# A fused S5 and SwiGLU layer: three input tiles on one queue, gate weights in three pieces, and a re-ordered first layer norm

## The chip, the cores and the metric

The kernel runs on one core of a Trainium2 chip. The metric is device time in microseconds (us) of one execution. The kernel before took 180.87 us (median of 4 runs, 180.3 to 181.23). The one execution that the profile was taken from took 181.51 us; its span, from the first to the last instruction, is 179.8 us, so 1.7 us lie around the span.

## What is computed

The input x is 2048 rows of 512 values in bfloat16. A layer norm over each row gives xn. The output is x plus two branches of xn:

```
xn  = layernorm(x)                                   # 2048 x 512
A   = 2 * Re(scan(B_bar xn)) @ C  + xn * Dskip       # complex diagonal recurrence over the 2048 rows, 512 states
B   = (silu(xn @ w_gate) * (xn @ w_up)) @ w_down     # 512 -> 1376 -> 512
out = x + A + B
```

## The kernel before, in words

The 2048 rows are 16 tiles of 128 rows, and four tiles make a chunk of 512 rows. TensorE needs xn transposed (features on partitions). For chunks 1 to 3 one DMA transpose per chunk does that (`xTd1` to `xTd3`, L556). For chunk 0 it is done by hand, so that TensorE can begin early:

- `ln_chunk0` (L509) normalises tiles 0 to 3 on VectorE. Per tile: two `bn_stats` on 256 columns each (`bn_half`, L500), one `bn_aggr` (L513), a square root on ScalarE (`sd`, L515), a reciprocal (L519), and the normalised tile in two halves of 256 columns (`ln_half`, L505). The chain of `order=(last,)` fixes the order on VectorE by hand: the first half statistics of tile a+1 stand ahead of the reciprocal of tile a, the second half statistics of tile a+1 behind both normalised halves of tile a.
- `xt_tile_fine` (L539) transposes one half tile with two TensorE transposes (L546) and copies the result to SBUF on ScalarE (`xTev`, L552).
- `ffn_gate_quarters` (L737) computes the first six 128-column blocks of the gate product for chunk 0, one quarter (one tile of 128 rows) at a time, two of the four K blocks per step (L760). The two transposes of tile q+1 stand inside quarter q, ahead of steps 8 and 10 of 12. Ahead of quarter 0 stand warm-up matmuls on a constant (L457).

After that come the up product of the same blocks (`ffn_up`, L715, evacuated by ScalarE at L785), the remaining gate and up blocks, the recurrence input (`ssm_b_chunk`, L832), and for each chunk the down product (L915) and the output product of the recurrence (L928). The recurrence itself runs on VectorE (L863 and L872). Its cos and sin tables and parameters are made in the first third (`params_a`, `params_b`, `tables`, L610 to L677).

Inputs come through DMAs that all go through `dma` (L378, issued at L387 or, for transposes, L382). SyncE issues nearly all of them in program order. Before the change ScalarE issues two: tile 1 of x and the first half of the gate weights (`ld_x1`, `ld_wgA0`). A DMA transpose waits for every DMA before it, and every DMA after a transpose waits for that transpose (L381, L385). So SyncE's queue is a serial chain once the first loads are done: two transposes of B, the transpose of chunk 1, two transposes of C, and only then the load of x for chunk 2 (`ld_x8`, L428).

The order of instructions on ScalarE, VectorE and GpSimd is not the program's. `_schedule` (L79) plays the program through with the cost `est` that each operation is given, and a DMA model of 330 bytes per ns and 2000 ns. At each step it takes the operation that can start first, or, among those within 200 ns of it, the one with the longest remaining chain (`bl`). TensorE and SyncE keep program order (`_CHAIN`). An `order` edge fixes a sequence without a semaphore. The order so planned is then fixed in the program, whatever the true times are.

The layer norm of chunk 2 is on this path: the statistics (L470, L474) on VectorE, `ve` and `rstd` on GpSimd (L478, L482), `nmr` on VectorE (L491), and the normalised tiles 8 to 11 on ScalarE (`xn8` to `xn11`, L494).

Of the kernel before, what the change touches and what calls it, by code (L numbers as in the profile page):

```python
# [14 lines left out]
AF = mybir.ActivationFunctionType  # L15
# [63 lines left out]
def _schedule(tasks, engines, slack=200.0):  # L79
    succ = defaultdict(list)  # L80
    for t in tasks:
        for d in t.deps | t.od:
            succ[d].append(t)
    chain_next = {}
    for eng in _CHAIN:
        lst = [t for t in tasks if t.eng == eng]
        for a, b in zip(lst, lst[1:]):
            chain_next[a] = b
    for t in tasks:
        t.lat = (_DMA_LAT + t.nbytes / _DMA_BW) if t.dma else 0.0  # L90
    for t in reversed(tasks):
# [12 lines left out]
    chain_pos = {e: 0 for e in _CHAIN}  # L104
    for e in engines:
        if e in _CHAIN:
            continue
        ready[e] = [t for t in remaining[e] if nun[t] == 0]
    free = {e: 0.0 for e in engines}
    dma_free = {e: 0.0 for e in engines}  # L110
    order = {e: [] for e in engines}
    left = len(tasks)
    done = set()

    def est_start(t, e):
        s = free[e]
        for d in t.deps:
            f = d.fin + _HOP
            if f > s:
                s = f  # L120
        return s

    while left:
        best = None
        for e in engines:
            if e in _CHAIN:
                lst = remaining[e]
# [110 lines left out]
def bass_parallel_sum__ssm_conv_s5__swiglu_ffn__prompt_kernel(  # L238
# [30 lines left out]
    g = _Graph()  # L269
    es = ExitStack()  # L270
    with es:
# [123 lines left out]
        TILEB = 128 * D * 2  # L395
        FH0 = 6 * 128

        def pload(name, slot, src):
            return dma(name, prow[4 * slot:4 * slot + 4, :], src.rearrange("(a p) -> a p", p=128), [("prow", slot)], 1024)
# [4 lines left out]
        def wg_load(h, **kw):  # L404
            return dma("ld_wgA%d" % h, wg[:, 2 * h:2 * h + 2, 0:FH0], wg_v[:, 2 * h:2 * h + 2, 0:FH0], [("wg", "a%d" % h)], 256 * FH0 * 2, **kw)
# [92 lines left out]

        def bn_half(a, h, order=()):
            return g.add("dve", lambda e: e.bn_stats(out=st0[:, a, h, :], in_=x_sb[:, a, h * 256:(h + 1) * 256]),  # L500
                         reads=[("x", a)], writes=[("st0", a, h)], name="bnst%d_%d" % (a, h), est=330, order=order)

        def ln_half(a, h, order=()):
            cs = slice(h * 256, (h + 1) * 256)
# [1 line left out]
                                                          op0=ALU.subtract, op1=ALU.mult),  # L506
                         reads=[("x", a), ("mv", a), ("rstd", a)], writes=[("xh", a, h)] + ([("xn", a % NXN)] if h else []), name="xn%d_%d" % (a, h), est=220, order=order)

        def ln_chunk0():  # L509
            last = bn_half(0, 0)  # L510
            for a in range(4):
                last = bn_half(a, 1, order=(last,))
                last = g.add("dve", lambda e, a=a: e.bn_aggr(out=mv[:, a, :], in_=st0[:, a].rearrange("p h s -> p (h s)")),  # L513
                             reads=[("st0", a, 0), ("st0", a, 1)], writes=[("mv", a)], name="bnag%d" % a, est=130, order=(last,))
                hold["sd"] = g.add("act", lambda e, a=a: e.activation(out=sd0[:, a:a + 1], in_=mv[:, a, 1:2], func=AF.Sqrt, bias=epst[:, 0:1]),  # L515
                                   reads=[("mv", a), ("epst",)], writes=[("sd0", a)], name="sd%d" % a, est=280)
                if a < 3:
                    last = bn_half(a + 1, 0, order=(last,))
                last = g.add("dve", lambda e, a=a: e.reciprocal(out=rstd[:, a:a + 1], in_=sd0[:, a:a + 1]), reads=[("sd0", a)], writes=[("rstd", a)],  # L519
                             name="rstd%d" % a, est=100, order=(last,))  # L520
# [18 lines left out]
        def xt_tile_fine(a, hs=(0, 1)):  # L539
            for h in hs:  # L540
# [13 lines left out]
                hold["evac"] = g.add("act", evac, reads=BK(slot), writes=[("xnTh", a, h)] + ([("xnT", 0, a % 4)] if h else []), name="xTev%d_%d" % (a, h), est=340)  # L554

        def xt_chunk_dma(c):  # L556
            s0 = (4 * c) % NXN
# [140 lines left out]

        def wres(nm, i):
            if nm == "wg" and i < 6:  # L700
                return [("wg", "a0"), ("wg", "a1")]
            return [(nm, 0 if i < 6 else 1)]

        FP = [(0, 2), (2, 2), (4, 2), (6, 2), (8, 2)]
# [32 lines left out]
        def ffn_gate_quarters(pairs):  # L737
# [2 lines left out]
            banks = {ip: next_pair() for ip in pairs}  # L740
            tiles = [(2 * ip + k, banks[ip] + k) for ip in pairs for k in range(2)]
            wbank, pbk = tiles[-2][1], tiles[-1][1]
            pe_warm(10, 512, wbank)
            ln_chunk0()
            xt_tile_fine(0, (0,))
            pe_warm(1, 256, wbank)
            xt_tile_fine(0, (1,))
            pe_warm(3, 128, wbank)
            for q in range(4):
                if q < 3:  # L750
                    steps = [(i, bk, 2 * kh, 2 * kh + 2) for kh in range(2) for i, bk in tiles]
                else:
                    steps = [(i, bk, 2 * kh, 2 * kh + 2) for kh in range(2) for i, bk in tiles[:2]] + [(i, bk, 0, 4) for i, bk in tiles[2:]]
                for n, (i, bk, k0, k1) in enumerate(steps):
                    if q < 3 and n in (8, 10):
                        xt_tile_fine(q + 1, ((n - 8) // 2,))

                    def mm(e, bk=bk, i=i, q=q, k0=k0, k1=k1):
                        for kt in range(k0, k1):
                            inst = e.matmul(pbank[:, bk, q * 128:(q + 1) * 128], lhsT=wg[:, kt, i * 128:(i + 1) * 128], rhs=xnT[:, 0, q, kt, :],  # L760
                                            start=(kt == 0), stop=(kt == KT - 1))
                        return inst
                    hs = range(k0 // 2, k1 // 2)
# [3 lines left out]
                    g.add("pe", mm, reads=[("wg", "a%d" % h) for h in hs] + [("xnTh", q, h) for h in hs], writes=BK(bk), name="mm_gq%d_%d_%d" % (i, q, k0),  # L767
                          est=(k1 - k0) * 56, ninst=k1 - k0)
            reserved.clear()
            act_table(AF.Silu, (hold["evac"],))  # L770
# [277 lines left out]
```

## Time and profile before

| what | value |
|---|---|
| median of 4 runs | 180.87 us (180.3 to 181.23) |
| the profiled execution | 181.51 us, span 179.8 us |
| busy in the span | TensorE 174.8 us (97%), VectorE 161.9 us (90%), ScalarE 89.4 us (50%) |
| first gate matmul | 7.40 us |
| first up matmul | 14.03 us |
| granted TensorE clock | 1.0 as the mean of the span |

How to read it: times are microseconds from the start of the span. PE is TensorE, PEld its weight loads, DVE VectorE, ACT ScalarE, POOL GpSimd, SP SyncE. An entry of a timeline gives the start, the time from the first start to the last end of the merged instructions, the engine, the line, the operation, output and input, the count, and in brackets how long the engine was idle before it and what ended that. TensorE's instructions overlap in a pipeline, so the time of a row of N matmuls is read from the starts of this row and the next.

### The profile page before, as it was taken

The numbers are of one execution on the slowest core, as the hardware profiler recorded it, in microseconds if no ns is written. First come the engines' busy times: TensorE is split into PE (matmuls) and PEld (weight loads), VectorE is DVE, ScalarE is ACT, GpSimd is POOL, SyncE is SP. The second block draws the span as 40 slices with busy tenths as digits, with TensorE's granted clock in tenths as the row PEclk, the third lists the DMA queues.
The fourth block names the chain that finished last, engine by engine and source line by source line (L and its number), as shares of the span: only waits on it lengthen the run. The fifth ranks groups of instructions, "written<-read, shape, count | busy, mean of one in ns | idle before, by whom it ended". The sixth has DMA issues, their size and how long they took to land.

```text
span 179.8 us, 2391 instructions
## 1 busy us (share of the span) xinstructions
PE 174.8 (97%) x917; PEld 83.5 (46%) x925; DVE 161.9 (90%) x280; ACT 89.4 (50%) x116; POOL 9.9 (6%) x21
## 2 busy tenths in 40 slices
PE   8799999999999999999999999999999999999994
PEld 2585444444444444444444444444444444444743
DVE  2759895697799999999999999999999999999983
ACT  3369989989799966106656552000865620000000
POOL 3005400000500000040000000000000000000000
PEclk9999999999999999999999999999999999999999
DMA  5993677569541000001250000001100000000122
GB/s 177 358 327 62 108 103 113 115 133 360 175 94 26 0 0 0 0 0 62 81 95 0 0 0 4 0 0 58 58 0 4 0 0 0 0 0 4 58 80 95
DMA packets 22882, 12.37 MB, mean 69 GB/s; under 512 B 15096, under 2 KB 22872, under 8 KB 22872
## 3 DMA queue, kind: packets, MB, share of 16 engines
q1 hardware_dynamic: 22456, 11.70, 25.4%
q10 hardware_dynamic: 416, 0.52, 0.9%
q8 instruction: 7, 0.11, 0.3%
q14 instruction: 3, 0.02, 0.1%
HBM read 6.46 MB, written 2.10 MB: 48 GB/s over the span
## 4 chain that ended last, share of the span: by engine, by line
PE 93%; DMA 3%; ACT 1%; issue 0%; ACTq 0%; DVE 0%
PE pb L715 35%; PE pb L915 21%; PE pb L832 15%; PE pb L928 15%; DMA wg<-in_B_w_gate_dram 3%; PE pb L760 3%; PE pb L795 2%; PE pb L805 1%; ACT xn_sb L494 1%; ACT uf L785 1%; PE pb L546 0%; ACTq L387 0%; DVE x_sb L933 0%; PE pb L462 0%
## 5 line engine op out<-in xcount | busy, mean ns | idle before, releaser
L872 DVE TENSOR_TENSOR_SCAN rot<-sm,car,rot 128x512 bf16<-128x512 f32 x32 | 39.0, 1266 | 0.1
L915 PE MATMUL pb<-wd,hT 128*128 128x512 bf16 (+3 forms) x194 | 38.1, 355 | 0.2
L715 PE MATMUL pb<-xnT,wu 128*128 128x512 bf16 x160 | 37.3, 379 | 0.1
L715 PE MATMUL pb<-xnT,wg 128*128 128x512 bf16 x136 | 32.0, 379 | 0.0
L928 PE MATMUL pb<-W,hss 128*128 128x512 bf16 (+2 forms) x140 | 28.1, 355 | 0.2
L832 PE MATMUL pb<-xnT,BT 128*128 128x512 bf16 x128 | 28.1, 379 | 0.0
L915 PEld LDWEIGHTS pb<-wd,hT 128*128 128x128 bf16 (+1 forms) x198 | 18.5, 98 | 19.9
L715 PEld LDWEIGHTS pb<-xnT,wu 128*128 128x128 bf16 x160 | 15.5, 98 | 19.1 <-ACT uf L785 0.6
L727 ACT ACTIVATE sg<-pb 128x1024 bf16<-128x1024 f32 x20 | 20.2, 1023 | 7.6 <-PE pb L715 7.5
L785 ACT ACTIVATE uf<-pb 128x1024 bf16<-128x1024 f32 x20 | 20.4, 1026 | 7.0 <-PE pb L715 6.8
L715 PEld LDWEIGHTS pb<-xnT,wg 128*128 128x128 bf16 x136 | 13.1, 98 | 16.4 <-issue 0.8
L928 PEld LDWEIGHTS pb<-W,hss 128*128 128x128 bf16 x144 | 13.5, 98 | 14.3
L832 PEld LDWEIGHTS pb<-xnT,BT 128*128 128x128 bf16 x128 | 12.5, 98 | 15.1
L839 ACT ACTIVATE u_sb<-pb 128x1024 bf16<-128x1024 f32 x16 | 16.4, 1025 | 4.8 <-PE pb L832 4.5
L787 DVE TENSOR_TENSOR hT<-sg,uf 128x1024 bf16<-128x1024 bf16 x20 | 13.3, 680 | 0.4 <-ACT uf L785 0.3
L863 DVE TENSOR_TENSOR rot<-u_sb,cosT 128x2048 bf16<-128x2048 bf16 x8 | 9.7, 1218 | 2.9 <-ACT cosT L676 2.9
L933 DVE TENSOR_TENSOR x_sb<-pb,x_sb 128x512 bf16<-128x512 f32 (+2 forms) x18 | 10.8, 622 | 1.3 <-PE pb L928 1.3
L814 ACT ACTIVATE sg<-pb 96x1024 bf16<-96x1024 f32 x2 | 2.0, 1020 | 17.3 <-PE pb L795 17.3
L494 ACT ACTIVATE xn_sb<-x_sb,nmr,rstd 128x512 bf16<-128x512 bf16 x8 | 5.9, 802 | 9.3 <-DVE nmr L491 9.3
L863 DVE TENSOR_TENSOR rot<-rot,cosT 128x2048 bf16<-128x2048 bf16 x8 | 9.7, 1217 | 0.1
L863 DVE TENSOR_TENSOR rot<-rot,sin 128x2048 bf16<-128x2048 bf16 x8 | 9.7, 1218 | 0.0
L863 DVE TENSOR_TENSOR rot<-u_sb,sin 128x2048 bf16<-128x2048 bf16 x8 | 9.7, 1217 | 0.0
(76 smaller groups left out, 142.7 us busy)
## 6 DMA issues: line engine op xcount, KB each, us to landing
out_dram<-x_sb SPq DMA_DIRECT2D x15, 128.0 KB, 1.7
x_sb<-in_A_x_dram SPq DMA_DIRECT2D x3, 512.0 KB, 7.5
wd<-in_B_w_down_dram SPq DMA_DIRECT2D x1, 1280.0 KB, 7.1
wu<-in_B_w_up_dram SPq DMA_DIRECT2D x1, 768.0 KB, 5.7
wg<-in_B_w_gate_dram SPq DMA_DIRECT2D x1, 608.0 KB, 7.1
wu<-in_B_w_up_dram SPq DMA_DIRECT2D x1, 608.0 KB, 8.2
x_sb<-in_A_x_dram SPq DMA_DIRECT2D x3, 128.0 KB, 3.3
wg<-in_B_w_gate_dram ACTq DMA_DIRECT2D x1, 384.0 KB, 6.0
```

The lines of the kernel that those rows point to most:

```text
L494: g.add("act", lambda e, a=a: e.activation(out=xn_sb[:, a % NXN, :], in_=x_sb[:, a, :], func=AF.Identity, scale=rstd[:, a:a + 1], bias=nmr ...
L715: inst = e.matmul(pbank[0:fs, bk, :].rearrange("p (j t) -> p j t", j=4), lhsT=w[:, kt, i * 128:i * 128 + fs], rhs=xnT[:, c % 2, :, kt, :], ...
L727: g.add("act", lambda e: e.activation(out=sg[rows, sl, 0:n, :].rearrange("p a t -> p (a t)"), in_=pair_f32(rows, bk, 512 * n), func=AF.Sil ...
L785: g.add("act", lambda e: e.activation(out=uf[rows, ul, 0:n, :].rearrange("p a t -> p (a t)"), in_=pair_f32(rows, bk, 512 * n), func=AF.Ide ...
L787: g.add("dve", lambda e: e.tensor_tensor(out=hT[rows, hb, i0:i0 + n, :], in0=sg[rows, sl, 0:n, :], in1=uf[rows, ul, 0:n, :], op=ALU.mult), ...
L832: inst = e.matmul(pbank[:, bk, :].rearrange("p (j t) -> p j t", j=4), lhsT=BT[:, ri, kt, pt * 128:(pt + 1) * 128], rhs=xnT[:, c % 2, :, kt ...
L839: g.add("act", lambda e: e.activation(out=u_sb[:, us].rearrange("p r t -> p (r t)"), in_=pair_f32(slice(0, 128), b0), func=AF.Identity), r ...
L863: tt = lambda out, a, b, op, r, w, nm: g.add("dve", lambda e: e.tensor_tensor(out=out, in0=a, in1=b, op=op), reads=r, writes=w, name="%s_% ...
L872: g.add("dve", lambda e, A0=A0, A1=A1, k=k, ri=ri, pt=pt: e.tensor_tensor_scan(out=A1[:, k, ri, :], data0=rr[:, pt:pt + 1].to_broadcast([1 ...
L915: inst = e.matmul(pbank[:, bk, 0:nc_], lhsT=hT[0:fs, hb, i, lt * 128:(lt + 1) * 128], rhs=wd[0:fs, i, c0:c0 + nc_], start=(i == 0), stop=F ...
L928: inst = e.matmul(pbank[:, bk, 0:nc_], lhsT=hss[:, hb, pt, ri, lt * 128:(lt + 1) * 128], rhs=W12[:, ri, pt, c0:c0 + nc_], start=False, sto ...
L933: g.add("dve", lambda e, bk=bk, a=a, c0=c0, nc_=nc_: e.tensor_tensor(out=x_sb[:, a, c0:c0 + nc_], in0=pbank[:, bk, 0:nc_], in1=x_sb[:, a, ...
```

## The change

It has five parts.

1. Tile 1 of x moves from ScalarE's queue to SyncE's, behind tile 0.
2. ScalarE's queue now begins with the small load of `log_dt` (1 KB), then K blocks 0 and 1 of the gate weights (384 KB), then K block 2 (192 KB). K block 3 (192 KB) is on SyncE behind tile 2. Before, blocks 2 and 3 were one load of 384 KB on SyncE. Quarter 0 of the gate product takes K blocks 2 and 3 in separate steps (18 steps in place of 12), and tile 1's transposes stand ahead of steps 12 and 15.
3. Tile 0's statistics are one `bn_stats` on 512 columns. On VectorE the second half statistics and the aggregation of tile a+1 now stand ahead of the second normalised half of tile a, and the first half statistics of tile a+2 behind it.
4. On ScalarE, by `order` edges: `sd1` ahead of the copy of tile 0's second half, `sd2` behind the copy of tile 1's second half, `sd3` behind the copy of tile 2's second half.
5. The first warm-up is nine matmuls of 512 columns and two of 128 in place of ten of 512. Four costs that the planner is given rise (330 to 350, 130 to 160, 100 to 140 ns; 640 for the full statistics). `_schedule` walks the graph in topological order, since an edge can now point to an operation made earlier.

```diff
-            return dma("ld_wgA%d" % h, wg[:, 2 * h:2 * h + 2, 0:FH0], ...)
+            return dma("ld_wg" + nm, wg[:, k0:k1, 0:FH0], wg_v[:, k0:k1, 0:FH0], [("wg", nm)], (k1 - k0) * 128 * FH0 * 2, **kw)
         x_load(0)
-        act_q = [x_load(1, eng="act")]
-        act_q.append(wg_load(0, eng="act", order=(act_q[-1],)))
+        x_load(1)
+        act_q = [pload("ld_ldt", 2, A_log_dt, eng="act")]
+        act_q.append(wg_load("a0", 0, 2, eng="act", order=(act_q[-1],)))
         x_load(2)
-        wg_load(1)
+        act_q.append(wg_load("a1", 2, 3, eng="act", order=(act_q[-1],)))
+        wg_load("a2", 3, 4)
         x_load(3)
-        pload("ld_ldt", 2, A_log_dt)
...
+        def ln_stat0(a, order):
+            t = g.add("dve", lambda e: e.bn_aggr(out=mv[:, a, :], in_=st0[:, a].rearrange("p h s -> p (h s)")[:, 0:6 if a == 0 else 12]),
+                      reads=[("st0", a, 0), ("st0", a, 1)], writes=[("mv", a)], name="bnag%d" % a, est=160, order=order)
+            hold["sd%d" % a] = g.add("act", lambda e: e.activation(out=sd0[:, a:a + 1], in_=mv[:, a, 1:2], func=AF.Sqrt, bias=epst[:, 0:1]), ...)
+            return t
         def ln_chunk0():
-            last = bn_half(0, 0)
+            last = g.add("dve", lambda e: e.bn_stats(out=st0[:, 0, 0, :], in_=x_sb[:, 0, :]), reads=[("x", 0)], writes=[("st0", 0, 0)], name="bnst0", est=640)
+            last = ln_stat0(0, (last,))
+            last = bn_half(1, 0, order=(last,))
             for a in range(4):
...
-                if a < 3:
-                    last = bn_half(a + 1, 0, order=(last,))
-                last = g.add("dve", lambda e, a=a: e.reciprocal(...), est=100, order=(last,))
-                for h in range(2):
-                    last = ln_half(a, h, order=(last,))
+                last = g.add("dve", lambda e, a=a: e.reciprocal(...), est=140, order=(last,))
+                last = ln_half(a, 0, order=(last,))
+                if a < 3:
+                    last = bn_half(a + 1, 1, order=(last,))
+                    last = ln_stat0(a + 1, (last,))
+                last = ln_half(a, 1, order=(last,))
+                if a < 2:
+                    last = bn_half(a + 2, 0, order=(last,))
...
-                hold["evac"] = g.add("act", evac, ..., est=340)
+                hold["evac"] = g.add("act", evac, ..., est=340,
+                                     order=(hold["sd1"],) if (a, h) == (0, 1) else ())
+                if (a, h) in ((1, 1), (2, 1)):
+                    hold["sd%d" % (a + 1)].od.add(hold["evac"])
...
-            pe_warm(10, 512, wbank)
+            pe_warm(9, 512, wbank)
+            pe_warm(2, 128, wbank)
...
-                if q < 3:
+                if q == 0:
+                    steps = [(i, bk, 0, 2) for i, bk in tiles] + [(i, bk, k, k + 1) for k in (2, 3) for i, bk in tiles]
+                elif q < 3:
...
-                    if q < 3 and n in (8, 10):
-                        xt_tile_fine(q + 1, ((n - 8) // 2,))
+                    if q < 3 and n in ((12, 15) if q == 0 else (8, 10)):
+                        xt_tile_fine(q + 1, (0 if n in (8, 12) else 1,))
```

More of the change, by code (lines that the diff above doesn't have):

```diff
@@ L90, in _schedule @@
         t.lat = (_DMA_LAT + t.nbytes / _DMA_BW) if t.dma else 0.0
-    for t in reversed(tasks):
+    nin = defaultdict(int)
+    for t in tasks:
+        for d in succ[t]:
+            nin[d] += 1
+    for d in chain_next.values():
+        nin[d] += 1
+    topo = [t for t in tasks if nin[t] == 0]
+    for t in topo:
+        for d in succ[t] + ([chain_next[t]] if t in chain_next else []):
+            nin[d] -= 1
+            if nin[d] == 0:
+                topo.append(d)
+    for t in reversed(topo):
         b = 0.0
@@ L396, in bass_parallel_sum__ssm_conv_s5__swiglu_ffn__prompt_kernel, with pload, wg_load @@
         FH0 = 6 * 128
-        def pload(name, slot, src):
-            return dma(name, prow[4 * slot:4 * slot + 4, :], src.rearrange("(a p) -> a p", p=128), [("prow", slot)], 1024)
+        def pload(name, slot, src, **kw):
+            return dma(name, prow[4 * slot:4 * slot + 4, :], src.rearrange("(a p) -> a p", p=128), [("prow", slot)], 1024, **kw)
         def x_load(a, **kw):
             return dma("ld_x%d" % a, x_sb[:, a:a + 1, :], x_v[:, a:a + 1, :], [("x", a)], TILEB, **kw)
-        def wg_load(h, **kw):
-            return dma("ld_wgA%d" % h, wg[:, 2 * h:2 * h + 2, 0:FH0], wg_v[:, 2 * h:2 * h + 2, 0:FH0], [("wg", "a%d" % h)], 256 * FH0 * 2, **kw)
+        def wg_load(nm, k0, k1, **kw):
+            return dma("ld_wg" + nm, wg[:, k0:k1, 0:FH0], wg_v[:, k0:k1, 0:FH0], [("wg", nm)], (k1 - k0) * 128 * FH0 * 2, **kw)
         x_load(0)
-        act_q = [x_load(1, eng="act")]
-        act_q.append(wg_load(0, eng="act", order=(act_q[-1],)))
+        x_load(1)
+        act_q = [pload("ld_ldt", 2, A_log_dt, eng="act")]
+        act_q.append(wg_load("a0", 0, 2, eng="act", order=(act_q[-1],)))
         x_load(2)
-        wg_load(1)
+        act_q.append(wg_load("a1", 2, 3, eng="act", order=(act_q[-1],)))
+        wg_load("a2", 3, 4)
         x_load(3)
-        pload("ld_ldt", 2, A_log_dt)
         pload("ld_lim", 1, A_Lambda_im)
@@ L500, in bn_half @@
             return g.add("dve", lambda e: e.bn_stats(out=st0[:, a, h, :], in_=x_sb[:, a, h * 256:(h + 1) * 256]),
-                         reads=[("x", a)], writes=[("st0", a, h)], name="bnst%d_%d" % (a, h), est=330, order=order)
+                         reads=[("x", a)], writes=[("st0", a, h)], name="bnst%d_%d" % (a, h), est=350, order=order)
         def ln_half(a, h, order=()):
@@ L507, in ln_half @@
                          reads=[("x", a), ("mv", a), ("rstd", a)], writes=[("xh", a, h)] + ([("xn", a % NXN)] if h else []), name="xn%d_%d" % (a, h), est=220, order=order)
+        def ln_stat0(a, order):
+            t = g.add("dve", lambda e: e.bn_aggr(out=mv[:, a, :], in_=st0[:, a].rearrange("p h s -> p (h s)")[:, 0:6 if a == 0 else 12]),
+                      reads=[("st0", a, 0), ("st0", a, 1)], writes=[("mv", a)], name="bnag%d" % a, est=160, order=order)
+            hold["sd%d" % a] = g.add("act", lambda e: e.activation(out=sd0[:, a:a + 1], in_=mv[:, a, 1:2], func=AF.Sqrt, bias=epst[:, 0:1]),
+                                     reads=[("mv", a), ("epst",)], writes=[("sd0", a)], name="sd%d" % a, est=280)
+            return t
@@ L509, in ln_chunk0 @@
         def ln_chunk0():
-            last = bn_half(0, 0)
+            last = g.add("dve", lambda e: e.bn_stats(out=st0[:, 0, 0, :], in_=x_sb[:, 0, :]), reads=[("x", 0)], writes=[("st0", 0, 0)], name="bnst0", est=640)
+            last = ln_stat0(0, (last,))
+            last = bn_half(1, 0, order=(last,))
             for a in range(4):
[L512 to L516, printed above, removed]
-                if a < 3:
-                    last = bn_half(a + 1, 0, order=(last,))
-                last = g.add("dve", lambda e, a=a: e.reciprocal(out=rstd[:, a:a + 1], in_=sd0[:, a:a + 1]), reads=[("sd0", a)], writes=[("rstd", a)],
-                             name="rstd%d" % a, est=100, order=(last,))
-                for h in range(2):
-                    last = ln_half(a, h, order=(last,))
@@ new lines, in ln_chunk0 @@
+                last = g.add("dve", lambda e, a=a: e.reciprocal(out=rstd[:, a:a + 1], in_=sd0[:, a:a + 1]), reads=[("sd0", a)], writes=[("rstd", a)],
+                             name="rstd%d" % a, est=140, order=(last,))
+                last = ln_half(a, 0, order=(last,))
+                if a < 3:
+                    last = bn_half(a + 1, 1, order=(last,))
[3 more added lines that the diff above has]
+                    last = bn_half(a + 2, 0, order=(last,))
@@ L553, in evac @@
                                         in_=ptr[:, slot, 0:256].rearrange("p (k t) -> p k t", k=2), func=AF.Identity)
-                hold["evac"] = g.add("act", evac, reads=BK(slot), writes=[("xnTh", a, h)] + ([("xnT", 0, a % 4)] if h else []), name="xTev%d_%d" % (a, h), est=340)
+                hold["evac"] = g.add("act", evac, reads=BK(slot), writes=[("xnTh", a, h)] + ([("xnT", 0, a % 4)] if h else []), name="xTev%d_%d" % (a, h), est=340,
+                                     order=(hold["sd1"],) if (a, h) == (0, 1) else ())
+                if (a, h) in ((1, 1), (2, 1)):
+                    hold["sd%d" % (a + 1)].od.add(hold["evac"])
         def xt_chunk_dma(c):
@@ L700, in wres @@
             if nm == "wg" and i < 6:
-                return [("wg", "a0"), ("wg", "a1")]
+                return [("wg", "a0"), ("wg", "a1"), ("wg", "a2")]
             return [(nm, 0 if i < 6 else 1)]
@@ L762, in mm @@
                         return inst
-                    hs = range(k0 // 2, k1 // 2)
+                    hs = range(k0 // 2, (k1 + 1) // 2)
                     if q == 3 and n == 4:
@@ L766, in ffn_gate_quarters @@
                         params_ev(xt_pair[0], (hold["xn3"],))
-                    g.add("pe", mm, reads=[("wg", "a%d" % h) for h in hs] + [("xnTh", q, h) for h in hs], writes=BK(bk), name="mm_gq%d_%d_%d" % (i, q, k0),
+                    g.add("pe", mm, reads=[("wg", "a%d" % max(k - 1, 0)) for k in range(k0, k1)] + [("xnTh", q, h) for h in hs], writes=BK(bk), name="mm_gq%d_%d_%d" % (i, q, k0),
                           est=(k1 - k0) * 56, ninst=k1 - k0)
```

## The prediction

> **What bounds the kernel now.** I read the chain of waits in order of time first. Its columns are start, duration, what.
>
> ```profile
> 1.22 6.04 DMA wg<-in_B_w_gate_dram
> 7.26 0.14 issue
> 7.40 1.05 PE pb L760 x16
> ...
> 42.80 6.51 PE pb L715 x30
> 49.31 1.41 ACT xn_sb L494 x2
> 50.72 0.92 ACT uf L785
> 51.63 0.05 issue
> 51.68 8.81 PE pb L715 x40
> ```
>
> Two things stand outside TensorE on it. The first is the load of the gate weights until 7.26, which the change attacks. The second is at 51.68, where TensorE waits for ScalarE (L785 behind L494). So I asked what sets 51.68, in the timelines of SyncE, VectorE, GpSimd and ScalarE.
>
> ```profile
> 14.92 2.13 SPq L382 DMA_TRANSPOSE BT<-in_A_B_re_dram  x1
> 19.61 2.58 SPq L382 DMA_TRANSPOSE BT<-in_A_B_im_dram  x1
> 25.03 1.84 SPq L382 DMA_TRANSPOSE xnT<-xn_sb  x1
> 29.31 2.40 SPq L382 DMA_TRANSPOSE hss<-in_A_C_re_dram  x1
> 34.04 1.57 SPq L382 DMA_TRANSPOSE hss<-in_A_C_im_dram  x1
> 38.47 0.37 SPq L387 DMA_DIRECT2D x_sb<-in_A_x_dram  x1
> ...
> 42.01 2.47 DVE L470 BATCH_NORM_STATS2 st<-x_sb 128x6 f32<-128x512 bf16 x4 [1.12 <-DMA x_sb<-in_A_x_dram]
> 45.51 1.85 POOL L482 TENSOR_TENSOR rstd<-ve,mhalf 128x4 f32<-128x4 f32 x1
> 47.47 0.16 DVE L491 SCALAR_TENSOR_TENSOR nmr<-mv,rstd 128x4 f32<-128x4 f32 x1 [0.94 <-POOL rstd L482]
> 47.79 2.93 ACT L494 ACTIVATE xn_sb<-x_sb,nmr,rstd 128x512 bf16<-128x512 bf16 x4 [1.00 <-DVE nmr L491]
> ```
>
> The reader is to see one serial chain without a TensorE instruction: the first loads end (tile group 4 to 7, issued at 5.70, lands 8.8 us later, at 14.5), five DMA transposes follow each other, x for chunk 2 is issued at 38.47 and lands at 42.0, VectorE had waited 1.12 us for it, and statistics, GpSimd and ScalarE follow back to back until 51.62. TensorE itself was ready at 49.65 + 8 x 0.216 = 51.38, with 0.216 from 24 matmuls in the 5.17 us from 14.03 to 19.20. It **waited 0.30 us** at 51.68. From there it runs to the end, so an earlier TensorE in the first 50 us only waits longer there.
>
> VectorE is tied to the same load, and it has little room at the end:
>
> ```profile
> 167.59 2.35 DVE L863 TENSOR_TENSOR hss<-rot 128x2048 bf16<-128x2048 bf16 x2
> 170.33 7.11 PE L928 MATMUL pb<-W,hss 128*128 128x512 bf16 x47
> ```
>
> The last recurrence output is ready at 169.94, and TensorE needs it at 170.33: 0.39 us. Between 60 and 150 us VectorE is busy 89.5 of 90 us (the busy times by stretch). Both engines would have to move for the end to move forward.
>
> **The change, part by part.** All in the profiled execution's own time.
>
> *Start of the gate product, loads.* The 384 KB on ScalarE's queue are issued at 1.22 in both, since a small load takes the place of tile 1's load, and 128 KB less stand ahead. In the DMA view cut into half microseconds, ScalarE's queue had moved 0.50 of its 0.52 MB by 5.0, then 3 or 4 packets per half microsecond until 7.0: the landing at 7.26 was that of a few stragglers. Bounds for the new landing: 3.9 (1.22 plus the 2.7 that tile 1 took) and 7.26. I take 6.0, nearer the late end, because the stragglers share engines with the same bytes. The two pieces of 192 KB lie between 6.0 and 7.4 (the old second half took 5.7 from 1.71); they are needed at 7.0 and 7.3, so they cost between nothing and 0.4.
>
> *Start, norm of tile 0.* Statistics 3.39 to 4.07 (0.68 for 512 columns, the L470 group), aggregation to 4.25 (0.17), root 4.29 to 4.58 (0.29), reciprocal to 4.78 (0.16), first half 4.81 to 5.16 (0.35). Then tile 1's second half statistics (0.42) and aggregation (0.21) stand ahead of the second half, which ends at 6.00 where it ended at 5.55. Transposes, three warm-ups, and the first gate matmul is at 6.35: **1.05 us earlier** than 7.40.
>
> *Ring through tiles 2 and 3.* This gives it back. `sd2` now stands behind the copy of tile 1's second half, and `sd3` behind that of tile 2. Tile 1's second half ends at 7.74 (VectorE runs through: half statistics 0.41, normalised halves 0.35). Its transposes start at 7.83, the copy is 8.14 to 8.52 (0.31 after the transposes, as 8.29 to 8.60), `sd2` 8.42 to 8.71, reciprocal to 8.91, first half of tile 2 8.94 to 9.29 (before 9.40 to 9.75), statistics and aggregation of tile 3 to 9.87, second half of tile 2 to 10.12 (before 10.01). Again: transposes 10.21, copy to 10.90, `sd3` to 11.09, tile 3's halves to 11.67 and 11.92 (before 11.75), last copy to 12.81 (before 12.63). The rest of quarter 3 takes 1.34 (12.68 to 14.03), so the first up matmul comes at 14.2 in place of 14.03. TensorE stalls at tile 2's two transposes and at tile 3's first. Bounds: 12.98 without any stall (four quarters of 1.65 from 6.35), 14.6 if the loads cost 0.4 more. I take 14.1 to 14.2.
>
> *What reaches 51.68.* TensorE would be ready there at 51.5, against 51.68. Anything from 1.05 earlier to 0.30 later is hidden; if the chain of transposes were not there, the cost would be 0.1 to 0.2.
>
> *The chain of transposes.* It moves only if the first loads end at another time. The bytes are the same. ScalarE's queue starts its large load 0.43 later (1.22 against 0.79), while SyncE's stays full: between 0 and 0.2 later, half the engines' time in that gap; I take 0.1. There is one more semaphore to wait for ahead of the first transpose. Between the landing at 14.5 and 14.92 lie the other twelve waits, 0.36 us or 0.06 a pair, in an order that the program doesn't fix; so from -0.3 to +0.06, I take 0. Issues on SyncE ahead of the first large up load: seven before, seven after.
>
> *Warm-up.* Nine of 512 and two of 128 end at 4.9 instead of 5.1 (0.43 each by the row of ten in 4.43 us); TensorE then waits for tile 0 as before, so it costs nothing. The records show the half rate until the 256-column matmul at 5.61, which was followed by the next after 0.21, and the full rate from 6.00 on, with 0.056 between 128-column matmuls. The Trainium skill (TensorE: Matmul & The Clock Gate, Part 1) speaks against shortening it: the clock rises only after a busy window of about 3.4 us that runs free of the kernel. If the gap that now opens ahead of tile 0's second half spoiled that window, the next would end 3.4 us later. By that page the matmuls from 6.35 to about 9.3 would run at half rate, and the sum for the first up matmul would be up to 1.5 later; by the row, with a gap before 5.44 already in the window, nothing.
>
> *The planner.* Its order for VectorE, ScalarE and GpSimd follows its own costs. By these (ring: root 280, reciprocal 140, halves 220, half statistics 350, aggregation 160, transposes 128, copy 340, hops of 60) I find chunk 0's gate product ending 0.94 us later in the plan than before, and the DMAs 0.07 earlier. So work tied to TensorE and work tied to loads shift by 1.01 against each other, and some neighbours swap: the statistics of tiles 4 to 7 go ahead of small parameter operations (hidden, the first table operation at 18.66 waits for ScalarE), and one table function (0.62, L670) goes behind L494 (hidden by ScalarE's idle 50%). Cost 0 to 0.8, see the second rival; I take 0.1.
>
> *Sum.* 0.1 (chain) + 0.1 (order) = +0.2 on 181.51. The profiled run lies 0.64 above the median of the runs, which is the measure, so 180.87 + 0.15 = **181.0 us**.
>
> **Rivals.**
>
> 1. *The early start reaches the end: 179.9 us.* It needs the chain of transposes to move too: if the first loads end with the bulk instead of the stragglers (the queue's bulk was done 2 us before 7.26), the first transpose starts up to 0.7 earlier, and by a better order of the waits another 0.3. For: VectorE and TensorE hang on that chain alone. Against: the bytes and their last queue are unchanged. 180.87 - 1.0 = 179.9.
>
> 2. *Slower, through VectorE's order: 181.8 us.* In the plan the scan that ran at 39.61 starts 1.27 us ahead of the statistics of x for chunk 2; the planner swaps them when the distance falls under its 0.2. That is from a shift of 1.07, and I find 1.01. Swapped, VectorE stands idle until 42.0 and owes a scan of 1.19 afterwards (two in a row take 2.45, one 1.27); 0.39 of it is covered at 170.33, 0.80 is not. 180.87 + 0.15 + 0.8 = 181.8.
>
> 3. *The change doesn't start the gate earlier*, because the stragglers hold the pieces until 7.3. Then the first up matmul comes at up to 14.6, and TensorE is ready for its work of 51.68 at 51.95: 0.3 later at most, 181.2, within the forecast.
>
> **How the numbers follow.** Forecast with rival 3: 0.66, 180.3 to 181.5 (the waits' -0.3 and the load's late end with the order's small losses). Rival 1: 0.14; rival 2 with its variants: 0.20. Taking most of both into the range gives 180.0 to 181.9. A difference of under 0.5% (0.9 us: 179.97 to 181.77) is about what a measurement of this kernel can't tell from no change. Rival 1 falls mostly outside: faster 0.13. Rival 2 does by a little more than half, with 0.04 for a larger loss: slower 0.16. Same 0.71.
>
> **What would show it.** In the profile after: first gate matmul near 6.35; ScalarE's copies with `sd2` and `sd3` behind them; VectorE's reciprocals at 8.7 and 11.1; the first up matmul near 14.1, not 13.0; the first transpose at 14.9 and x for chunk 2 at 42 within 0.3; the wait at L715 near 51.7 still there. Wrong if the first transpose moves by over 0.5 us, if L494 no longer stands ahead of L785, or if VectorE's last L863 ends after 170.3.

## The result and the profile after

Before: 181.05 us, median of 51 runs (180.3 to 182.1). After: 181.42 us, median of 32 runs (180.83 to 182.74). The ratio is 1.0022, with a 95% interval of 1.0011 to 1.0033: 0.2% slower, inside the forecast's "same" and its range of 180.0 to 181.9, 0.4 above the forecast of 181.0. Two later executions (185.18 us in experiment 3, 183.39 in experiment 7) lie more than 1.5% above the fastest of their kernel and are left out of the ratios. The profiled execution of after took 181.43 us with a span of 179.7, that of before 181.51 with 179.8. The cost of the change is thus not in the difference of these two traces; it took further runs to find it.

First the serial chain in the profile after, from the timelines of SyncE, VectorE, ScalarE and TensorE (start, time, engine, line, operation; in brackets the idle time before it and what ended it).

```profile
13.72 1.90 SPq L394 DMA_TRANSPOSE BT<-in_A_B_re_dram  x1
18.04 2.19 SPq L394 DMA_TRANSPOSE BT<-in_A_B_im_dram  x1
22.41 1.78 SPq L394 DMA_TRANSPOSE xnT<-xn_sb  x1
27.52 1.96 SPq L394 DMA_TRANSPOSE hss<-in_A_C_re_dram  x1
33.54 2.05 SPq L394 DMA_TRANSPOSE hss<-in_A_C_im_dram  x1
37.99 0.37 SPq L399 DMA_DIRECT2D x_sb<-in_A_x_dram  x1
...
47.06 0.16 DVE L504 SCALAR_TENSOR_TENSOR nmr<-mv,rstd 128x4 f32<-128x4 f32 x1 [0.94 <-POOL rstd L495]
47.67 2.93 ACT L507 ACTIVATE xn_sb<-x_sb,nmr,rstd 128x512 bf16<-128x512 bf16 x4 [1.57 <-DVE nmr L504]
51.55 1.90 PE L738 MATMUL pb<-xnT,wu 128*128 128x512 bf16 x8 [0.20 <-ACT uf L811]
```

The same chain is there, and TensorE still waits for it near 51.6. Three things differ. The first transpose comes 1.20 us earlier (13.72 against 14.92) and, after two shorter transposes of B, that of chunk 1 2.62 earlier (22.41 against 25.03). Two transposes then give nearly all of it back: chunk 1 takes 5.11 us to the next issue (22.41 to 27.52) where it took 4.28, and the real part of C 6.02 (27.52 to 33.54) where it took 4.73 (29.31 to 34.04). So x for chunk 2 is issued only 0.48 earlier. And ScalarE starts L507 0.45 us after VectorE's L504 has ended (47.22 to 47.67); before, it was 0.16 (47.63 to 47.79).

The front, which is TensorE's work up to the first up matmul, from the timelines of ScalarE and TensorE:

```profile
7.61 0.66 ACT L572 ACTIVATE xnT<-pb 128x256 bf16<-128x256 bf16 x2 [1.21 <-PE pb L566]
8.17 0.29 ACT L525 ACTIVATE sd<-mv,epst 128x1 f32<-128x1 f32 x1
10.21 0.39 ACT L572 ACTIVATE xnT<-pb 128x256 bf16<-128x256 bf16 x1 [0.41 <-PE pb L566]
10.49 0.28 ACT L525 ACTIVATE sd<-mv,epst 128x1 f32<-128x1 f32 x1
...
6.10 1.36 PE L786 MATMUL pb<-xnT,wg 128*128 128x128 bf16 x18
13.85 0.59 PE L738 MATMUL pb<-xnT,wu 128*128 128x512 bf16 x2
```

The gate product starts at 6.10 (7.40 before), `sd2` and `sd3` stand behind the copies, and the first up matmul comes at 13.85 (14.03 before): of 1.30 us the ring (normalise a tile, transpose it, copy it, then the next tile's square root) leaves 0.18.

The end, from the timelines of VectorE and TensorE:

```profile
167.36 2.35 DVE L889 TENSOR_TENSOR hss<-rot 128x2048 bf16<-128x2048 bf16 x2
170.21 5.13 PE L954 MATMUL pb<-W,hss 128*128 128x512 bf16 x22
```

VectorE's last output is ready at 169.71, half a microsecond ahead of its use. It isn't the bound.

### The profile page after: what moved, and what is told of

Same layout as the page of the kernel before. It is cut to its first block, busy times and chain, and to the rows that moved or that the text cites. A ratio compares the mean times of both kernels' runs of the same rounds, so it can differ in the third digit from the quotient of the medians.

```text
span 179.7 us, 2393 instructions
## 1 busy us (share of the span) xinstructions
PE 175.3 (98%) x918; PEld 83.9 (47%) x926; DVE 161.8 (90%) x279; ACT 89.4 (50%) x116; POOL 9.6 (5%) x21
## 4 chain that ended last, share of the span: by engine, by line
PE 92%; ACT 3%; DVE 2%; ACTq 1%; issue 1%
PE pb L738 35%; PE pb L941 21%; PE pb L858 15%; PE pb L954 15%; PE pb L821 2%; PE pb L786 2%; PE pb L831 1%; DVE xn_sb L518 1%; ACTq L399 1%; ACT xn_sb L507 1%; ACT L459 1%; PE pb L566 1%; ACT xnT L572 1%; ACT uf L811 1%; DVE st L513 0%
## 5 line engine op out<-in xcount | busy, mean ns | idle before, releaser
L507 ACT ACTIVATE xn_sb<-x_sb,nmr,rstd 128x512 bf16<-128x512 bf16 x8 | 5.9, 803 | 9.8 <-DVE nmr L504 9.8
```

The source lines that it names most:

```text
L507: g.add("act", lambda e, a=a: e.activation(out=xn_sb[:, a % NXN, :], in_=x_sb[:, a, :], func=AF.Identity, scale=rstd[:, a:a + 1], bias=nmr ...
```

## The experiments

An instruction can wait for several semaphores. The planner collects these waits from a Python set, and the set's order decides which one wait sits in the instruction itself; the others become event instructions ahead of it. In the trace of before, ScalarE's wait for L491 sits in the first L494; in that of after it sits in the event instruction ahead of L507 (47.25 to 47.29), and the activation starts 0.38 us behind that. All experiments therefore sort the waits by the planner's times, so that only what is meant to differ differs:

```diff
-                for d in t.deps:
+                for d in sorted(t.deps, key=lambda d: (d.fin, d.idx), reverse=True):
```

With `reverse=True` the wait that comes last sits in the instruction. Each kernel was timed against the kernel before on the same chip.

**Experiment 1: before, last wait in the instruction.** The edit above alone.

> The kernel before, with one edit: the waits of an instruction are sorted by the planner's times, so that the wait that comes last always sits in the instruction itself and the others in the event instructions ahead of it. Theory (a serial chain of transposes, VectorE, GpSimd and ScalarE sets the end; TensorE's early start is hidden): the first transpose issues 0.36 us earlier, right at the landing of tiles 4 to 7; ScalarE's first normalisation of chunk 2 keeps its 0.16 us behind VectorE, as in before; TensorE's wait of 0.30 near 51.7 shrinks to about 0, so 180.7 (before: 181.05). Rival (the place of the waits is of no account): 181.05, ratio 1.000.

181.18 us (12 runs), ratio 0.9998 (0.9980 to 1.0016). The first transpose did move up, to 14.21, and ScalarE's 0.22 us behind VectorE is near the 0.16 of before, but the gain did not arrive (180.7 was expected): the real part of C took 6.00 us, and x for chunk 2 was issued at 38.34 (38.47 before). The run also showed something that I had not looked for, in TensorE's timeline:

```profile
6.27 1.28 PE L760 MATMUL pb<-xnT,wg 128*128 128x128 bf16 x16
13.14 1.24 PE L715 MATMUL pb<-xnT,wu 128*128 128x512 bf16 x5
...
51.56 1.90 PE L715 MATMUL pb<-xnT,wu 128*128 128x512 bf16 x8 [0.91 <-ACT uf L785]
```

With the same front as in before, the gate product starts at 6.27 and the first up matmul comes at 13.14. The 7.40 and 14.03 of the first profile belong to one execution with late weights: 15 of the 16 DMA engines that carry that load had signalled their end by 5.54, the last at 7.26. Here TensorE waits 0.91 near 51.6.

**Experiments 2 and 11: after, last wait in the instruction** (two measurements of one program, the second on the chip of experiment 12).

> The changed kernel with the same edit of the waits. Theory with the place of the waits as the cause of the measured +0.37: ScalarE's start behind VectorE goes from 0.45 us back to 0.16, so 181.1 or less, and within 0.15 us of the run of before with the same edit. Rival A (the planner's new order costs it: one table function behind the normalisation, one VectorE product moved by 6 us): 0.3 above the run of before with the same edit. Rival B (place of the waits of no account): 181.4.

> The kernel of the second experiment once more, on the chip of the twelfth: changed kernel, last wait in the instruction everywhere. Theory (only the place of ScalarE's wait and the start of the chain of transposes decide): 181.1 again, the end of the span 141.3 us behind the issue of x for chunk 2. Rival (the changed kernel loses something else): 181.4.

181.18 us both times (12 runs each), ratios 1.0014 (0.9992 to 1.0036) and 1.0014 (0.9994 to 1.0034). The median is that of experiment 1: with the waits sorted alike, the change as a whole and the planner's new order cost nothing at the median that these runs can tell from zero. Both profiled executions were late ones (181.95 and 183.00), for one reason. In experiment 11, timelines of SyncE and TensorE:

```profile
16.44 2.24 SPq L394 DMA_TRANSPOSE BT<-in_A_B_re_dram  x1
39.82 0.37 SPq L399 DMA_DIRECT2D x_sb<-in_A_x_dram  x1
...
53.13 1.90 PE L738 MATMUL pb<-xnT,wu 128*128 128x512 bf16 x8 [1.57 <-ACT uf L811]
```

Of the 16 signals (one from each engine) for the load of tiles 4 to 7, 15 had come at 14.50, the last at 16.43 (15.07 and 15.86 in experiment 2). TensorE waits 1.57 us for one late engine 37 us earlier.

**Experiment 3: after, last wait ahead of the instruction** (ascending order, so that the first wait sits in it).

> The changed kernel with the waits sorted the other way: the wait that comes first sits in the instruction, and the one that comes last in an event instruction ahead of it. Theory of the place of the waits: ScalarE starts its first normalisation of chunk 2 0.45 us behind VectorE, TensorE waits 0.3 longer near 51.6, and the run is 0.3 us slower than the one sorted the right way round. Rival (place of no account): the same time, within 0.1.

181.45 us (12 runs), ratio 1.0002 (0.9983 to 1.0022). ScalarE is 0.44 us behind VectorE. The median is 0.27 above experiment 2, as expected, but the intervals overlap. In the profiled execution the chain was fast (x for chunk 2 issued at 37.32), and TensorE did not wait near 51 at all: its own front (first up matmul at 13.61) set the end, at 179.07.

**Experiments 5 and 12: only the wait of one instruction moved**, on before and on after.

```diff
+                for d in sorted(t.deps, key=lambda d: (d.fin, d.idx), reverse=t.name != "xn8"):
```

> The kernel before with the waits sorted as in the first experiment (last one in the instruction), except for one instruction, ScalarE's first normalisation of chunk 2, whose wait for VectorE is put into the event instruction ahead of it. Theory (this wait's place is what the changed kernel's build paid): ScalarE starts it 0.44 us behind VectorE in place of 0.22, the end of the span lies 141.7 us behind the issue of x for chunk 2 (141.3 with the wait in the instruction), and the median goes from 181.18 to 181.4. Rival (something else made the 0.4): 141.3 again and 181.15.

> The changed kernel with the last wait in the instruction everywhere except at ScalarE's first normalisation of chunk 2, as in the fifth experiment, but on the changed kernel. Theory: 0.25 us slower than the eleventh experiment, at 181.35, with ScalarE 0.44 us behind VectorE and the end of the span 141.6 us behind the issue of x for chunk 2. Rival (the place is of no account): the same as the eleventh, within 0.1.

Experiment 5: 181.41 us (12 runs), ratio 1.0010 (0.9997 to 1.0022), 0.23 above experiment 1. Experiment 12: 181.36 us (12 runs), ratio 1.0026 (1.0004 to 1.0047), 0.18 above experiment 11. The rows say it plainly; first experiment 5, then 12 (timelines of VectorE and ScalarE):

```profile
47.20 0.17 DVE L491 SCALAR_TENSOR_TENSOR nmr<-mv,rstd 128x4 f32<-128x4 f32 x1 [0.86 <-POOL rstd L482]
47.80 2.93 ACT L494 ACTIVATE xn_sb<-x_sb,nmr,rstd 128x512 bf16<-128x512 bf16 x4 [1.82 <-DVE nmr L491]
```

```profile
46.60 0.16 DVE L504 SCALAR_TENSOR_TENSOR nmr<-mv,rstd 128x4 f32<-128x4 f32 x1 [0.86 <-POOL rstd L495]
47.20 2.93 ACT L507 ACTIVATE xn_sb<-x_sb,nmr,rstd 128x512 bf16<-128x512 bf16 x4 [1.43 <-DVE nmr L504]
```

From VectorE's end to ScalarE's start it is 0.43 to 0.45 us in all four traces with the wait ahead (after, 3, 5, 12) and 0.16 to 0.22 in all five with the wait in the instruction and the chain as it was (before, 1, 2, 4, 11). The end of the span follows: from the issue of x for chunk 2 it is 141.27 to 141.43 us in these five, and 141.54 to 141.68 in after, 5 and 12 (in 3 the front sets the end). That the place costs about 0.25 us on the chain is shown. That the medians rise by it is likely (three pairs, all with the same sign: 0.27, 0.23, 0.18), though no pair settles it alone, experiment 3 turned every wait round and not one, and experiments 1 and 5 ran on different chips.

**Experiment 4: after without the two edges on the square roots.**

```diff
-                if (a, h) in ((1, 1), (2, 1)):
-                    hold["sd%d" % (a + 1)].od.add(hold["evac"])
```

> The changed kernel, waits sorted with the last one in the instruction, and without the two order edges that put the square roots of tiles 2 and 3 behind the copies of the second halves of tiles 1 and 2. Theory (TensorE's start is hidden behind the chain): the first up matmul comes 0.5 to 1.0 us earlier than the 13.85 of the changed kernel, TensorE waits that much longer near 51.6, and the time is within 0.15 us of the changed kernel with the same waits. Rival (the ring's loss is what the change pays for): 0.5 to 1.0 us faster.

180.95 us (12 runs), ratio 0.9987 (0.9968 to 1.0007). From TensorE's timeline:

```profile
5.99 1.17 PE L784 MATMUL pb<-xnT,wg 128*128 128x128 bf16 x18
12.87 1.67 PE L736 MATMUL pb<-xnT,wu 128*128 128x512 bf16 x7
51.11 1.90 PE L736 MATMUL pb<-xnT,wu 128*128 128x512 bf16 x8 [0.72 <-ACT uf L809]
```

The first up matmul comes at 12.87, 0.98 earlier than in after and 0.91 earlier than in experiment 2, and TensorE waits 0.72 near 51.1. The median is 0.23 below that of experiments 2 and 11, a little more than the 0.15 of the theory and far from the 0.5 to 1.0 of the rival; the intervals overlap.

**Experiments 6, 7 and 8: the chain's last link taken out.** x for chunk 2 is loaded ahead of the two transposes of C; the order of ScalarE, VectorE and GpSimd is held to what it was.

```diff
         def loads_stage_b2():
+            dma("ld_x8", x_sb[:, 8:12, :], x_v[:, 8:12, :], [("x", a) for a in range(8, 12)], 4 * TILEB)
             dma("ld_cre", CT[:, 0], A_C_re, [("CT", 0)], 512 * 512 * 2, xpose=True)
             dma("ld_cim", CT[:, 1], A_C_im, [("CT", 1)], 512 * 512 * 2, xpose=True)
-            dma("ld_x8", x_sb[:, 8:12, :], x_v[:, 8:12, :], [("x", a) for a in range(8, 12)], 4 * TILEB)
```

> The kernel before, last wait in the instruction, with x for chunk 2 loaded two transposes earlier (ahead of the two of C); the order of ScalarE, VectorE and GpSimd is kept as it was. Theory (the chain through this load sets the end): its landing no longer matters, VectorE loses its wait for it, TensorE runs through near 51 and starts the next stage when it is ready, at 50.6 to 51.4 in place of 51.6; time 180.2 to 181.0, with less spread from run to run. Rival (VectorE's own order sets the end): 181.15, unchanged, with VectorE's last recurrence output as late as before.

> The changed kernel with the same two edits. Theory: TensorE is ready near 51.2 and runs through; now its own start counts, so the time is 180.8, and it lies 0 to 0.6 behind the kernel before with the same edit, since the first up matmul came at 13.14 there (with last waits in the instruction) and at 13.8 here. Rival (the start of the gate product is worth its 1 us once it is not hidden): 0.5 to 1.0 faster than the kernel before with the same edit.

> The changed kernel with the same two edits and without the two edges that hold the square roots of tiles 2 and 3 behind copies. Theory: first up matmul at 12.9, TensorE ready near 50.4 and not held by the chain: 180.0, about 0.9 faster than the changed kernel with the load moved alone. Rival (VectorE becomes the bound as soon as TensorE is early): no better than 180.7, with TensorE waiting for the last recurrence outputs near 160 to 170.

Experiment 6 (before): 180.43 us (5 runs, 180.30 to 180.61), ratio 0.9959 (0.9946 to 0.9973). Experiment 7 (after): 180.86 us (12 runs), ratio 0.9982 (0.9971 to 0.9994). Experiment 8 (after, no edges): 180.00 us (6 runs), ratio 0.9943 (0.9925 to 0.9962). No wait is left near 51 in any of the three. TensorE's timeline of experiment 6 and of experiment 8:

```profile
6.81 1.07 PE L765 MATMUL pb<-xnT,wg 128*128 128x128 bf16 x16 [0.78 <-DMA wg<-in_B_w_gate_dram]
13.45 1.03 PE L720 MATMUL pb<-xnT,wu 128*128 128x512 bf16 x4
50.80 1.89 PE L720 MATMUL pb<-xnT,wu 128*128 128x512 bf16 x8
```

```profile
5.91 1.17 PE L789 MATMUL pb<-xnT,wg 128*128 128x128 bf16 x18
12.66 1.89 PE L741 MATMUL pb<-xnT,wu 128*128 128x512 bf16 x8
50.01 1.89 PE L741 MATMUL pb<-xnT,wu 128*128 128x512 bf16 x8
```

From the first up matmul to the start at 50, both take 37.35 us. Now the front reaches the end. As it stands, the change is 0.43 us slower than before (7 against 6); without its two edges it is 0.43 faster (8 against 6). The traces of 6 and 7 don't show this difference, since both reach the up matmul at 13.45: the one of 6 is the slowest of its five runs, with a wait of 0.78 for weights. Without the edges the planner's order also goes back towards the old one; but from 7 to 8 the span falls by as much as the up matmul (13.45 to 12.66), so no other cost of that order is left to see.

**Experiments 9 and 10: the parts of the change alone**, both on experiment 6: first its loads (parts 1 and 2, with the shortened warm-up), then its order of the norm (parts 3 and 4) without the two edges.

> The kernel before with the two edits of the sixth experiment (last wait in the instruction, x for chunk 2 early), and of the change only the loads: tiles 0 to 2 on SyncE, the gate weights in three pieces behind the small load, the gate product's first quarter in the pieces' steps, the shortened warm-up; the order of the norm as in before. Theory (with the chain out of the way the time is the first up matmul plus 165.45 of span and 1.75): no wait for weights, gate product from 5.9, first up matmul near 12.7 by the 6.87 that the kernel before took between the two, 179.9. Rival (the new order of the norm is what makes the ring fast without the edges): up matmul at 13.2 or later, 180.4.

> The kernel before with the two edits of the sixth experiment, and of the change only the new order of the norm (next tile's statistics ahead of the second normalised half), without the two edges; the loads as in before. Theory (the loads make the front earlier, the order of the norm does nothing for it): gate product at 6.4 to 6.8, held by the gate weights, first up matmul at 13.2 to 13.5, 180.4 as in the sixth experiment. Rival (the order of the norm shortens the ring): up matmul at 12.9 or earlier, 180.0.

Experiment 9: 180.02 us (5 runs), ratio 0.9935 (0.9923 to 0.9947), gate product from 5.94 with a wait of 0.16 for weights (none was expected), first up matmul at 12.82: otherwise as expected. Experiment 10: 180.21 us (5 runs), ratio 0.9946 (0.9932 to 0.9960), gate product from 6.25, first up matmul at 12.90. Here the theory was wrong: the weights had landed at 5.05 and held nothing, and the rival was right on the up matmul. In time the order of the norm alone gains about 0.2 over experiment 6, but on another chip, and the two ratios' intervals overlap. The two gains don't add: with both parts it is 180.00. The loads alone bring the whole of it. Experiments 8 and 9 are the best versions, some 1 us (0.6%) faster than the kernel before, and most of that comes from the one moved load.

**What the end follows.** In experiments 6 to 10 the span is the first up matmul plus 165.45 us (165.44 to 165.46 in all five). In before, the span is the issue of x for chunk 2 plus 141.3; with the wait ahead I take 141.6 (experiment 12). Then the later of the two sums should be the span; the rows of before and 12 gave the constants, the other seven test them:

| run | up matmul + 165.45 | issue of x + 141.3 (141.6) | span |
|---|---|---|---|
| before | 179.48 | 179.77 | 179.78 |
| after | 179.30 | 179.59 | 179.68 |
| 1 | 178.59 | 179.64 | 179.66 |
| 2 | 179.23 | 180.24 | 180.22 |
| 3 | 179.06 | 178.92 | 179.07 |
| 4 | 178.32 | 179.18 | 179.22 |
| 5 | 178.72 | 179.84 | 179.78 |
| 11 | 179.50 | 181.12 | 181.25 |
| 12 | 179.04 | 179.18 | 179.19 |

The rows agree to 0.13 us or better, over spans that differ by 2.2.

## Why the prediction was right, and where it was not

*The bound* was right: a chain of transposes ahead of x for chunk 2, with TensorE's front hidden behind it. Experiments 6 to 8 show it.

*Start of the gate product.* Predicted 6.35, measured 6.10 (5.89 to 6.10 in eight traces of the change with or without its edges). The weights' landing was mis-sized: taken 6.0, it was 4.98, all 16 signals without a late one, and the last two pieces did not hold TensorE. The norm of tile 0 was mis-sized too: VectorE began at 2.93, 0.46 earlier than I took it, since tile 0 landed at 2.90. So 6.35 came out 0.25 late through two terms.

*The ring.* Predicted to give back nearly all through the two edges, 7.8 us from gate to up matmul; measured 7.75. The terms were right: `sd2` at 8.17 (8.42 predicted) and `sd3` at 10.49 (10.80) stand behind the copies. Experiment 4 shows the cause: without the edges it takes 6.88.

*The base was wrong.* I held 14.2 against 14.03 and called the front a small loss. Before's front, in its other traces, reaches the up matmul at 13.14, 13.27 and 13.45. The changed one needs 13.45 to 14.05. So the changed front is some 0.4 us later, not 0.15 (experiments 6 and 7 differ by 0.43), and of the 1.30 us by which the gate product starts earlier, 0.6 to 1.1 was one late engine in one execution: in its other traces before starts it at 6.27 to 6.81. This matters as soon as the chain is fast, as in experiment 3: 13.61 + 165.45 + 1.75 (the profiled time less its span) = 180.81, and the lowest run of after is 180.83; 13.14 gives 180.34, and the lowest of before is 180.30.

*The chain's start.* I took +0.1. It was -1.20 in the trace of after. With the changed loads it is at 13.64 to 14.07 in seven traces and late by one engine (15.88, 16.44) in two; with the old ones 14.21 to 14.92 in four and 13.49 in one. So it is typically half a microsecond earlier, and late in two of nine. In the trace of after, 0.83 of the 1.20 is the landing of tiles 4 to 7 (13.71 against 14.54) and 0.37 the wait behind it. This is what rival 1 needed, and it is the prediction's own sign of being wrong: a first transpose that moves by over 0.5 us. Its gain didn't come, because the transposes of chunk 1 and of C gave it back (next section) and because of ScalarE's wait. The prediction knew neither, so that the time stayed near the forecast is in this part luck.

*The order of the waits* is the step that failed. I had seen that the program doesn't fix it, but bounded it for SyncE alone (-0.3 to +0.06) and took 0. There it came out at -0.37: the first transpose started 0.38 us behind the landing before, 0.01 behind it after. The same freedom sits at ScalarE's first L507, on the chain, and costs 0.25 us there. The profiled execution of after has the bad place, that of before the good one. Which place each of the timed runs had, the traces don't tell.

*The planner's order.* As predicted, the table function went behind L507, the statistics of tiles 4 to 7 went ahead of the small parameter operations, and the scan stayed at 39.43, ahead of the statistics of chunk 2. The +0.1 isn't seen: experiments 1, 2 and 11 have the same median, within intervals of 0.3 to 0.4 us either way.

*Warm-up.* The trace of after is the one in which the half rate reached the gate product: 0.107 us between 128-column matmuls until 6.42, then 0.056. Four gate matmuls lost 0.05 each and four instructions ahead of them as much, 0.4 us together. In the twelve experiments the full rate was there before the first gate matmul. The Trainium skill (TensorE: Matmul & The Clock Gate, Part 1) calls this run-variable, since the window runs free; the traces agree that it varies (3.7 to 6.5 us). Eight of the nine traces with the shortened warm-up had the full rate in time; no run changed the warm-up alone.

*The sum.* Its two terms add up to 0.2, but 0.15 went into the forecast; by its own terms it is 181.1. The forecast was 0.4 low, 0.18 of that through the base: 180.87 was the median of 4 runs, 51 give 181.05. Of the measured +0.37, the place of one wait accounts for about 0.2 by the medians of experiments 5 and 12; the later front, which lifts the fastest runs, is my account for the rest. That division was not measured, and the runs show a third part: late executions. Seven of the 32 runs of after lie above 181.75 us, against one of the 51 of before. The place of the wait isn't what makes them: with the wait in the instruction (experiments 2 and 11) it is 6 of 24, in experiment 1 none of 12. The two of these that were profiled had a late engine in the load of tiles 4 to 7. Why the changed loads should meet it more often is open; experiment 4, with the same loads, has none in 12.

## Where the chain's earlier start went

In the nine traces with the old place of x for chunk 2, the real part of C takes 4.73 to 6.02 us to the next issue. From starts at 27.19 to 27.90 it takes 6.00 to 6.02 four times (after, 1, 3, 12) and 5.50 once (4); from starts at 28.57 to 29.95 it takes 4.73 to 5.27 (before, 2, 5, 11). So an early chain loses here most of what it had.

Each of these nine windows also holds one 16 KB transfer of an instruction queue (in the DMA views; it starts at 29.4 to 31.6 and takes 0.9 to 1.4 us). Roughly, the further into the transpose it begins, the longer the transpose: begun 0.32 to 0.12 us ahead of the transpose's first packets, 4.73 to 5.12 (before, 2, 5); 0.17 and 0.39 behind them, 5.50 and 5.27 (4, 11); 1.15 to 2.44 behind, 6.00 to 6.02 (after, 1, 3, 12). In after, 3 and 12 a single engine delivers the last signal about 1.55 us after the others. In experiments 6 to 10 that transfer begins in the plain load of x, and the same transpose takes 4.26 to 4.64; in experiment 6 it is over at 32.35, and the transpose's packets begin at 33.2.

Two other transposes in the same 14 traces point the same way. The imaginary part of B takes 4.89 to 5.35 us from issue to landing in the seven traces in which an 8 KB instruction transfer begins 0.5 us or more behind its first packets (5.35 in before), 4.36 in the one where it begins with them (9), and 4.09 to 4.72 in the six without one (4.36 in after). The transpose of chunk 1 takes 4.51 to 5.10 in the four with such a transfer inside (5.10 in after, with one engine 0.86 late), 4.22 and 4.31 in the two where it begins with the packets, and 4.23 to 4.27 in the eight without one. This fits a collision of the instruction transfer with the transpose, but no run moved the one without the other: it is argued from traces, not shown by an experiment.

## What to carry over

Take the base of a comparison from more than one execution when a load's last engine sets it: here the gate product's start in the profile of before was 0.6 to 1.1 us later than in its other traces. When the order of waits is free, look at every instruction on the critical chain, not only at the queue with the longest list, and put the wait that comes last into the instruction. And before tuning a front, take out the link that hides it: moving one load made 0.4% here, and only then could the parts of the change be told apart.

## Unexpected behaviour of the hardware

- A wait in an event instruction ahead of a ScalarE activation, in place of in the activation: 0.43 to 0.45 us against 0.16 to 0.22 from VectorE's end to ScalarE's start.
- A single DMA engine can be 0.8 to 1.9 us late (tiles 4 to 7: 15 signals by 14.50, the last at 16.43), and with a serial chain behind it the whole span moves. The Trainium skill (DMA: Bandwidth & Descriptors, Why a DMA increments its semaphore by 16 and not by 1) says that the engines of a transfer finish independently and the semaphore counts them; these rows agree and give the spread.
- The DMA transpose of the real part of C took up to 6.0 us with an instruction transfer begun inside it, 4.3 to 4.6 without one (not tested in isolation).
- The full TensorE rate came between 3.7 and 6.5 us from the span's start in programs whose warm-up began at the same 0.83.
